# The first stage of a spectral and feed-forward kernel rewritten: the order of statistics and tables, twiddles in two parts, one PSUM pool

## The chip, the cores and the metric

The kernel runs on one core of a Trainium2 chip. A core has four computing engines, each with its own instruction stream: TensorE (PE in the profile, with PEld for its weight loads), VectorE (DVE), ScalarE (ACT) and GpSimd (POOL). SyncE (SP) issues the DMAs. An engine takes its instructions in the order of the program and waits on semaphores for the others. The metric is the device time of one execution in microseconds (us). The kernel before took 509.39 us, the median of three runs (509.39, 510.88, 509.39).

## The reference

The input is one sequence of 2048 rows with 576 columns, in bfloat16. It goes through a spectral mixing layer and a gated feed-forward layer, each with a layer norm ahead of it and a residual sum behind it:

```
def layernorm(x): return (x - mean(x)) / sqrt(var(x) + 1e-5)      # over the 576 columns

def A(x, w_r, w_i):                                # x: 1 x 2048 x 576
    X = rfft2(x, axes=(-2, -1))                    # 2048 x 289 complex
    return irfft2(X * (w_r + 1j * w_i), s=(2048, 576)).astype(bfloat16)

def B(x, w_gate, w_up, w_down):                    # 576 x 4608 twice, 4608 x 576
    return (gelu(x @ w_gate) * (x @ w_up)) @ w_down

h   = x + A(layernorm(x), A_w_r, A_w_i)
out = h + B(layernorm(h), B_w_gate, B_w_up, B_w_down)
```

## The kernel before

The 2048 rows are held as 128 partitions by 16 rows (`h_sb`, index h). The transform along the rows is done as a product of small transforms, all as matmuls with tables of sines and cosines that the kernel makes itself at its start.

**Preparation** (to about 14 us). SP loads the input in five chunks, then the spectral weights WR and WI and the first three groups of feed-forward weights (`pre`). POOL writes index patterns with iota (`iu`, `ic`, `ip`, `iD`, `iJ`, `ik`, `rev`), makes the identity, and clears DF, DI and, later, three `Zt` tiles. VectorE works out angles from them: `mu` for the 16-point table F16, `s2p` for the twiddles, `pd` and `kd` (L221 to L230) for the column tables. ACT turns angles into sines.

**First stage** (about 14 to 30 us), for the 16 rows h. The mean and variance of a row come either from VectorE (`sd`, which calls `ln_dve`: three instructions, L120 to L122; ten of the rows) or from ACT (`ln_act`: two activations that also sum, L127; rows 1, 3, 5, 7, 9, 11), after which POOL finishes them (`ln_fin`, L131 to L133). POOL also makes the reciprocal of the standard deviation for a group of rows (`ln_rstd`: an addition, L137, and a power, L138). VectorE normalises a row into `xn` (`normalise`, L141). PE multiplies it with F16 (`row16`): four matmuls into `f2t` (L261) and two small ones into `f4` (L270). `fill` (L249) adds matmuls whose results are overwritten: 30 ahead of row 0, one ahead of each of rows 1 to 11, and four ahead of the first channel. ACT moves the results from PSUM into `Bt` (`evict`, L280, two rows at a time; `evict4`, L286, four rows of the small ones). PSUM is in one pool with three double banks for `f2t` and two single ones for `f4`, closed after this stage; a second pool with four double banks follows.

The order of these calls is written out by hand, row by row (L315 to L370):

```
    sd(0, 2)                       # L325, then F16, ln_rstd(rstd, mv, 0, 4)
    norms(0, 4)                    # L338: normalise and row16 of rows 0 to 3
    ln_rstd(rstd, mv, 4, 8)
    sd(8, 10)
```

**Column tables.** `col_sin` makes the sines and cosines of the columns in DT (two of three blocks of 128 columns) and D3 (the third); DF, DI and DS are rearranged copies, some by DMA (`sine_rows`).

**Twiddles.** After the rows, VectorE works out the angles of nine channels in one piece (L373 to L376) and ACT makes the sines (L377) and, inside the loop's first turn, the cosines (L383, `twiddles`), both in TF. A DMA transposes TF into TI (L384), and another then loads `wd_a`.

**Channel loop** (L625, about 30 to 64 us), in the order 1 to 7, then 0, in which each channel c is taken together with c + 8. `f2` multiplies Bt with the column tables (L456) and moves the result to `pq` (L464: ACT, VectorE for channel 9). `f3` applies the twiddles TF (`comb`, L471 and L472) and ACT moves g and hs out (L492). `sums_of` adds and subtracts them into `xab` (L501, L502); `wmul` multiplies with WR and WI (L519 to L531) into a `Zt` tile. `i3` applies the transposed twiddles TI (L547, L549). The steps of three channels overlap: in turn i the loop issues f2 of channel i, f3 of channel i-1, wmul of channel i-2 and i3 of channel i-3. `weights()` (L404 to L407), called in the first turn, finishes WR and WI on VectorE. `late_tables()` (L410 and following) is called in the second.

**The rest.** `inv_cols` is the inverse transform of the columns (L596); after that the second layer norm, whose rows are transposed by DMA, and the feed-forward part (L848 and L868), from 78.67 us to the end.

Of the kernel before, what the change touches and what calls it, by code (L numbers as in the profile page):

```python
# [20 lines left out]
P = 128  # L21
# [20 lines left out]
def kernel_body(  # L42
# [33 lines left out]
    chunks = ((0, 2), (2, 4), (4, 8), (8, 12), (12, 16))  # L76
# [31 lines left out]
    DT = keep.tile([P, 2, 2, 2, JH], BF16, name="DT")  # L108
# [20 lines left out]
    def ln_fin(dst, h):  # L129
        sq = roll.tile([P, 1], FP32, name="sq", tag="sq", bufs=2)  # L130
        G.tensor_scalar(dst[:, h, :], sums[:, h, :], 1.0 / D, None, op0=ALU.mult)  # L131
        G.tensor_tensor(sq[:], dst[:, h, 0:1], dst[:, h, 0:1], ALU.mult)
        G.tensor_tensor(dst[:, h, 1:2], dst[:, h, 1:2], sq[:], ALU.subtract)  # L133
# [42 lines left out]
    def iota(t, pattern, base=0, cm=0):  # L176
        G.iota(t, pattern=pattern, base=base, channel_multiplier=cm, allow_small_or_imprecise_dtypes=True)

    iu, ic = tmp("iu", [P, H, 8]), tmp("ic", [P, H, 8])
# [6 lines left out]
    iota(ip[:], [[0, 1]], 0, 1)  # L186
    iD = tmp("iD", [P, 3], FP32)
# [3 lines left out]
    make_identity(nc, ident[:])  # L191
    rev = tmp("rev", [P, 1])
    iota(rev[:], [[0, 1]], 2 * P - 1, -2)
    G.memset(DF[:], 0.0)
    G.memset(DI[:], 0.0)
    ik = tmp("ik", [P, 9, P], FP32)
    iota(ik[:], [[1, 9], [16, P]])

# [18 lines left out]


    V.tensor_scalar(iD[64:128, 2:3], iD[64:128, 2:3], 192.0, None, op0=ALU.add)
    pd, kd = tmp("pd", [P, 3, JP], FP32), tmp("kd", [P, 3, JP], FP32)  # L220
    V.tensor_tensor(  # L221
        pd[:],
        iD[:, :].unsqueeze(2).to_broadcast([P, 3, JP]),
        iJ[:, :].unsqueeze(1).to_broadcast([P, 3, JP]),
        ALU.mult,
    )
    C23 = 8388608.0
    V.tensor_scalar(kd[:], pd[:], 1.0 / D, C23, op0=ALU.mult, op1=ALU.add)
    V.tensor_scalar(kd[:], kd[:], -C23, -float(D), op0=ALU.add, op1=ALU.mult)
    V.tensor_tensor(pd[:], kd[:], pd[:], ALU.add)  # L230

    def drop_sign(dst, src):
        V.tensor_scalar(
            dst[:].bitcast(I32),
            src[:].bitcast(I32),
            1,
            1,
            op0=ALU.logical_shift_left,
            op1=ALU.logical_shift_right,
        )  # L240

# [9 lines left out]
    def row16(h):  # L251
        if h % 2 == 0:
            ps_f[h] = two("f2t")
        if h % 4 == 0:
            ps_f["f4", h] = one("f4")
        f2t, f4 = ps_f[h - h % 2], ps_f["f4", h - h % 4]
        fill(f2t[:, h % 2, :], 30 if h == 0 else 1 if h < 12 else 0)
        x = xn[:, h, :]
        for t in range(2):
            for n, d0 in ((0, t * P), (1, DH + t * P)):  # L260
                T.matmul(  # L261
                    f2t[:, h % 2, t * 2 * P : (t + 1) * 2 * P],
                    lhsT=x[:, d0 : d0 + P],
                    rhs=F16[:, n : n + 2, :],
                    start=(n == 0),
                    stop=(n == 1),
                )
        o = (h % 4) * P
        for p0, d0 in ((0, 256), (64, 512)):
            T.matmul(  # L270
                f4[p0 : p0 + 64, o : o + P],
                lhsT=x[:, d0 : d0 + 64],
                rhs=F16[:, 0, :],
                start=True,
                stop=True,
            )

    def evict(*hs):
        for h in hs:
            A.copy(  # L280
                Bt[:, 0:4, :].rearrange("p t (c h l) -> p (t c) h l", c=16, h=16)[:, :, h : h + 2, :],
                ps_f[h][:].rearrange("p h (tc l) -> p tc h l", l=8),
            )

    def evict4(h):
        A.copy(  # L286
            Bt[:, 4, :].rearrange("p (c h l) -> p h c l", c=16, h=16)[:, h : h + 4, :, :],
            ps_f["f4", h][:].rearrange("p (h c l) -> p h c l", h=4, c=16),
        )
# [5 lines left out]
    def fin(*hs):  # L295
        for h in hs:
            ln_fin(mv, h)

# [5 lines left out]
    D3 = tmp("D3", [P, 2, 2, JH], BF16)  # L304
    pr, ab = tmp("pr", [P, 9, P]), tmp("ab", [P, 9, P], FP32)
# [4 lines left out]
    def col_sin(r, src, bias):  # L310
        s = src[:].rearrange("p t (a j) -> p t a j", a=2)
        A.activation(DT[:, :, :, r, :], s[:, 0:2], ACT.Sin, bias=bias[:], scale=-2.0 * PI / D)
        A.activation(D3[:, :, r, :], s[:, 2], ACT.Sin, bias=bias[:], scale=-2.0 * PI / D)

    for h in range(1, 12, 2):  # L315
        ln_act(h)
    fin(1, 3)
    for t, w in zip(wm, (A_w_r, A_w_i)):
# [6 lines left out]
    sd(0, 2)  # L325
    V.tensor_tensor(
        F16[:, 0:2, :],
        fs[:].unsqueeze(1).to_broadcast([P, 2, P]),
        mask[:].unsqueeze(1).to_broadcast([P, 2, P]),
        ALU.mult,  # L330
    )
    V.tensor_scalar(F16[:, 2, :], F16[:, 0, :], -1.0, None, op0=ALU.mult)
    ln_rstd(rstd, mv, 0, 4)
    for z in Zts:
        G.memset(z[:, :, J:], 0.0)
    sd(4, 6)
    fin(5, 7)
    norms(0, 4)  # L338
    ln_rstd(rstd, mv, 4, 8)
    sd(8, 10)  # L340
    fin(9, 11)
    col_sin(1, pd, zerob)
    drop_sign(kd, pd)
    norms(4, 6)
    evict(0)
    norms(6, 8)
    ln_rstd(rstd, mv, 8, 12)
    evict(2)
    evict4(0)
    evict(4)  # L350
    sd(14, 13)
    norms(8, 10)
    col_sin(0, kd, hpib)
    sd(12)
    norms(10, 12)
    ln_rstd(rstd, mv, 12, 14)
    sd(15)
    ln_rstd(rstd, mv, 14, 16)
    evict(6)
    evict4(4)  # L360
    evict(8)
    norms(12, 14)
    G.tensor_copy(DF[0:32], D3[0:32])
    G.tensor_copy(DF[96:128], D3[96:128])
    evict(10)
    evict4(8)
    norms(14, 16)
    evict(12)
    evict4(12)
    evict(14)  # L370


    V.tensor_scalar(pr[:], ik[:], s2p[:, 0:1], None, op0=ALU.mult)  # L373
    V.tensor_scalar(pr[:], pr[:], 2047, None, op0=ALU.bitwise_and)
    V.tensor_scalar(ab[:], pr[:], -1024.0, None, op0=ALU.add)
    drop_sign(ab, ab)  # L376
    A.activation(TF[:, :, 2, :], pr[:], ACT.Sin, bias=pib[:], scale=-2.0 * PI / S)  # L377
    V.tensor_scalar(TF[:, :, 0, :], TF[:, :, 2, :], -1.0, None, op0=ALU.mult)


    def twiddles():
        sine_rows()
        A.activation(TF[:, :, 1, :], ab[:], ACT.Sin, bias=nhpib[:], scale=2.0 * PI / S)  # L383
        nc.sync.dma_start(  # L384
            TI[:].rearrange("p k r q -> p (k r) q"), TF[:].rearrange("p k r q -> p (k r q)"), transpose=True
        )
        nc.sync.dma_start(wd_a[:], wd_view[:, 0:NWA, :])
# [41 lines left out]
    psum_pool.__exit__(None, None, None)  # L429
    psum = ctx.enter_context(tc.tile_pool(name="psum2", bufs=1, space=bass.MemoryType.PSUM))  # L430

    def two(name):
        return psum.tile([P, 2, 512], FP32, name=name, tag="two", bufs=4)

# [8 lines left out]
    order = [1, 2, 3, 4, 5, 6, 7, 0]  # L443

# [4 lines left out]
    def f2(c):  # L449
        ps = two("pq_ps")  # L450
        if c == 1:
            fill(ps[:, 0, :], 4)
# [17 lines left out]
    def comb(dst, k1, t0, a, t1, b):  # L470
        T.matmul(dst, lhsT=TF[:, k1, t0, :], rhs=a, start=True, stop=False)  # L471
        T.matmul(dst, lhsT=TF[:, k1, t1, :], rhs=b, start=False, stop=True)  # L472
# [62 lines left out]
    def i3(k, s):  # L535
# [7 lines left out]
        if k:  # L543
            pv = ps[:].rearrange("p a (n h e l) -> p (a n) e h l", n=2, h=H, l=8)
            for n, w in (((0, 0), (1, 1)), ((2, 3), (3, 4)), ((0, 2),))[s]:
                o = w * P
                T.matmul(pv[:, n], lhsT=z[:, o : o + P], rhs=TI[:, k, 1:3, :], start=True, stop=False)  # L547
                o += 2 * ZS
                T.matmul(pv[:, n], lhsT=z[:, o : o + P], rhs=TI[:, k, 0:2, :], start=False, stop=True)  # L549
# [13 lines left out]
        for n, c, j, p0, m in (  # L563
# [4 lines left out]
            for b in range(2):  # L568
                for a in range(2):
# [3 lines left out]
                        rhs=TI[:, 8 * b, 1 - a + c, :],  # L573
# [51 lines left out]
    for i in range(n + 1):  # L625
# [3 lines left out]
        if i == 0:  # L629
            twiddles()  # L630
# [14 lines left out]
        if not last:  # L645
            f2(order[i] + 8)
        if i == 0:
            weights()
# [285 lines left out]
```

## Time and profile before

| what | value |
|---|---|
| median of three runs | 509.39 us |
| time of the profiled execution | 509.37 us |
| its span in the trace | 507.2 us |
| PE busy | 494.9 us (98%) |
| VectorE busy | 214.7 us (42%) |
| ACT busy | 152.0 us (30%) |
| POOL busy | 32.6 us (6%) |
| first matmul of row 0 | 14.07 us |
| first matmul of the channel loop (f2) | 30.65 us |
| first matmul of the feed-forward part | 78.67 us |

The span runs from the first to the last record of the trace. A line of the timeline has the start in us, the duration in us, the engine, the line of the code, the operation, what it writes and reads, and how many instructions it stands for. A line of the chain of waits has start, length, engine, what is written, and the line; the chain is followed back from the last instruction to what released it.

### The profile page before, as it was taken

The numbers are of one execution on the slowest core, as the hardware profiler recorded it, in microseconds if no ns is written. First come the engines' busy times: TensorE is split into PE (matmuls) and PEld (weight loads), VectorE is DVE, ScalarE is ACT, GpSimd is POOL, SyncE is SP. The second block draws the span as 40 slices with busy tenths as digits, with TensorE's granted clock in tenths as the row PEclk, the third lists the DMA queues.
The fourth block names the chain that finished last, engine by engine and source line by source line (L and its number), as shares of the span: only waits on it lengthen the run. The fifth ranks groups of instructions, "written<-read, shape, count | busy, mean of one in ns | idle before, by whom it ended". The sixth has DMA issues, their size and how long they took to land.

```text
span 507.2 us, 9921 instructions
## 1 busy us (share of the span) xinstructions
PE 494.9 (98%) x4355; PEld 292.4 (58%) x4355; DVE 214.7 (42%) x418; ACT 152.0 (30%) x265; POOL 32.6 (6%) x81
## 2 busy tenths in 40 slices
PE   6989999999999999999999999999999999999997
PEld 2457775555557774444467744444577544444775
DVE  8979974689661015433311034433201233333001
ACT  8588984322230002333310023233200132323000
POOL 8700010111110000000000000000000000000000
PEclk9999999999999999999999999999999999999999
DMA  8985057779970019997730089978400577780000
GB/s 287 230 149 156 1 162 207 151 151 193 190 143 1 0 43 200 187 200 145 148 64 0 1 182 198 186 163 156 101 0 1 120 162 156 159 153 3 13 12 25
DMA packets 86811, 60.85 MB, mean 120 GB/s; under 512 B 22640, under 2 KB 85488, under 8 KB 86768
## 3 DMA queue, kind: packets, MB, share of 16 engines
q1 hardware_dynamic: 86480, 59.03, 57.7%
q0 software_dynamic: 288, 1.18, 0.9%
q8 instruction: 34, 0.56, 0.5%
q14 instruction: 9, 0.07, 0.1%
HBM read 52.65 MB, written 2.36 MB: 108 GB/s over the span
## 4 chain that ended last, share of the span: by engine, by line
PE 93%; DVE 4%; DMA 1%; ACT 1%; POOL 0%; issue 0%; ACTq 0%
PE gu L848 55%; PE acc L868 28%; PE f2t L261 2%; PE pq_ps L456 1%; PE cs_ps L596 1%; PE eo_ps L549 1%; PE y_ps L713 1%; PE eo_ps L547 1%; PE gh_ps L472 1%; PE f2t L249 1%; DMA Bt<-hrow 1%; PE gh_ps L471 1%; DMA h_sb<-in_A_x_dram 1%; PE f L270 1%; DVE h_sb L758 1%; DVE st L121 0%
## 5 line engine op out<-in xcount | busy, mean ns | idle before, releaser
L848 PE MATMUL gu<-Bt,wgu 64*128 64x512 bf16 x2592 | 281.5, 376 | 0.9 <-DMA Bt<-hrow 0.9
L848 PEld LDWEIGHTS <-wgu 64*128 64x128 bf16 x2592 | 130.9, 94 | 148.3 <-issue 1.9
L856 ACT ACTIVATE g_sb<-gu 128x512 f32<-128x512 f32 x144 | 86.0, 597 | 302.8 <-PE gu L848 302.8
L857 DVE TENSOR_TENSOR P_sb<-g_sb,gu 128x512 bf16<-128x512 f32 x144 | 98.7, 685 | 152.9 <-ACT g_sb L856 152.9
L868 PEld LDWEIGHTS <-P_sb 128*128 128x128 bf16 x1152 | 112.4, 98 | 30.6 <-issue 2.4
L868 PE MATMUL acc<-wd,P_sb 128*128 128x288 bf16 x768 | 99.3, 286 | 0.0
L880 DVE TENSOR_TENSOR h_sb<-h_sb,acc 128x576 bf16<-128x576 bf16 x15 | 11.3, 754 | 118.2 <-PE acc L868 118.2
L868 PE MATMUL acc<-wd_a,P_sb 128*128 128x288 bf16 x384 | 52.3, 286 | 0.5 <-DVE h_sb L876 0.5
L249 PE MATMUL f2t<-h_sb,ident 128*128 128x512 bf16 x41 | 13.2, 447 | 4.4 <-DMA h_sb<-in_A_x_dram 4.4
L456 PE MATMUL pq_ps<-DT,Bt 128*128 128x290 bf16 x64 | 12.4, 287 | 0.0
L738 DVE TENSOR_SCALAR hrow<-h_sb,mv,rstd 128x1152 bf16<-128x1152 bf16 x14 | 12.1, 866 | 0.0
L138 POOL TENSOR_TENSOR rstd<-rstd,mhalf 128x1 f32<-128x1 f32 (+2 forms) x17 | 11.8, 694 | 1.4
L249 PEld LDWEIGHTS <-ident 128*128 128x128 bf16 x45 | 4.9, 108 | 11.9 <-issue 5.9
L137 POOL TENSOR_SCALAR rstd<-mv 128x1 f32<-128x1 f32 (+2 forms) x17 | 4.1, 239 | 109.7 <-DVE mv L122 109.5
L596 PEld LDWEIGHTS <-EO 128*128 128x128 bf16 x96 | 9.1, 96 | 3.0 <-issue 0.2
L456 PEld LDWEIGHTS <-Bt 128*128 128x128 bf16 x96 | 9.2, 97 | 2.5
L261 PE MATMUL f2t<-F,xn 128*128 128x256 bf16 x64 | 9.7, 274 | 0.8 <-DVE xn L141 0.8
L464 ACT CAST pq<-pq_ps 128x580 bf16<-128x580 f32 x15 | 9.9, 660 | 0.9 <-PE pq_ps L456 0.8
L120 DVE BATCH_NORM_STATS2 st<-h_sb 128x6 f32<-128x288 bf16 x22 | 9.8, 444 | 0.0
L121 DVE BATCH_NORM_STATS2 st<-h_sb 128x6 f32<-128x288 bf16 x22 | 9.7, 442 | 0.0
L280 ACT CAST Bt<-f2t 128x1024 bf16<-128x1024 f32 x8 | 8.1, 1011 | 5.2 <-PE f2t L261 5.2
L596 PE MATMUL cs_ps<-DI,EO 128*128 128x290 bf16 x32 | 9.1, 285 | 0.0
(135 smaller groups left out, 263.3 us busy)
## 6 DMA issues: line engine op xcount, KB each, us to landing
wgu<-in_B_w_gate_dram SPq DMA_DIRECT2D x48, 432.0 KB, 5.2
wgu<-in_B_w_up_dram SPq DMA_DIRECT2D x48, 432.0 KB, 6.7
wd<-in_B_w_down_dram SPq DMA_DIRECT2D x2, 1728.0 KB, 7.9
h_sb<-in_A_x_dram SPq DMA_DIRECT2D x3, 576.0 KB, 5.9
wd_a<-in_B_w_down_dram SPq DMA_DIRECT2D x1, 1728.0 KB, 9.0
out_dram<-h_sb SPq DMA_DIRECT2D x3, 576.0 KB, 3.3
WR<-in_A_w_r_dram SPq DMA_DIRECT2D x1, 650.2 KB, 8.7
WI<-in_A_w_i_dram SPq DMA_DIRECT2D x1, 650.2 KB, 11.3
```

The lines of the kernel that those rows point to most:

```text
L138: G.tensor_tensor(dst[:, sl], dst[:, sl], mhalf[:, sl], ALU.pow)
L249: T.matmul(dst, lhsT=ident[:], rhs=h_sb[:, 2, 0:512], start=True, stop=True)
L261: T.matmul(f2t[:, h % 2, t * 2 * P : (t + 1) * 2 * P], lhsT=x[:, d0 : d0 + P], rhs=F16[:, n : n + 2, :], start=(n == 0), stop=(n == 1),)
L456: T.matmul(ps[:, par, 0:JP], lhsT=Bt[:, t, col], rhs=DT[:, t // 2, par] if t < 4 else DF[:, par], start=(t == par), stop=(t == 4),)
L464: (V.tensor_copy if c == 9 else A.copy)(sb[:].rearrange("p r (j a) -> p r j a", a=2), ps[:, :, 0:JP].rearrange("p a (r j) -> p r j a", r=2),)
L596: T.matmul(ps[:, e, 0:JP], lhsT=EO[x][:, 2 * e + jt if jt < 2 else 4, 2 * g : 2 * g + 2].rearrange("p h e k l -> p (h e k l)"), rhs=DI[:, ...
L738: V.tensor_scalar(hrow[:], h_sb[:, h, :].rearrange("p (r k) -> p r k", k=64).unsqueeze(2).to_broadcast([P, NR, 2, 64]), mv2[:, h, 0:1], rs ...
L848: T.matmul(gu[:, c, :], lhsT=w[rows, r, i * P : (i + 1) * P], rhs=hl[tcnk % 2][rows, r, :], start=(r == 0), stop=(r == NR - 1),)
L856: A.activation(g_sb[:], gu[:, 0, :], ACT.Gelu_apprx_tanh)
L857: V.tensor_tensor(p_sb(fa + i), g_sb[:], gu[:, 1, :], ALU.mult)
L868: T.matmul(acc[:, c, 0:DH], lhsT=p_sb(f)[:, st * P : (st + 1) * P], rhs=wd[f // NWA][:, f % NWA, cc], start=(f == 0), stop=(f == NFT - 1),)
L880: V.tensor_tensor(hv, hv, acc[:, :, 0:DH], ALU.add)
```

## The change

Preparation. DF, DI and the `Zt` tiles are cleared on VectorE, ahead of `mu`, instead of on POOL. The 1152-element pattern `ik` is replaced by a 9-element `kv` and a 128-element `q16`. `pd` and `kd` are made later, in two functions (`turns`, `phases`) with per-partition scalars in place of broadcast operands. The input is loaded in six chunks.

Statistics. `ln_act` scales inside the activation and sums straight into `mv`; `ln_fin` then takes two POOL instructions for two rows instead of three for each. `ln_act` calls are spread between the evictions. The first `ln_rstd` is issued ahead of POOL's two indirect DMAs instead of behind them.

Twiddles. They are made in two parts, for the channels in the order in which the loop uses them (`ts`): the first two ahead of the rows, the other seven in turns 0 to 2 of the loop. Each part has its own transposing DMA.

Rows. `fill` has 16 matmuls ahead of row 0 instead of 30, and five behind the last row instead of four in `f2(1)`. The small matmuls of rows 12 to 15 (`row16_rest`) come after the large ones; rows 14 and 15 are evicted one by one; the last `evict4` and the DF copies are on VectorE. D3 becomes the third block of DT, so that `col_sin` is one activation. All PSUM tiles come from one pool of four double banks. `weights()` and `sine_rows()` are called ahead of the loop, and `f2(9)` follows `f2(1)` directly.

```diff
-    psum_pool = tc.tile_pool(name="psum", bufs=1, space=bass.MemoryType.PSUM)
-    psum = psum_pool.__enter__()
+    psum = ctx.enter_context(tc.tile_pool(name="psum", bufs=1, space=bass.MemoryType.PSUM))
...
-        return psum.tile([P, 2, 512], FP32, name=name, tag="two", bufs=3)
-
-    def one(name):
-        return psum.tile([P, 512], FP32, name=name, tag="one", bufs=2)
+        return psum.tile([P, 2, 512], FP32, name=name, tag="two", bufs=4)
...
-    chunks = ((0, 2), (2, 4), (4, 8), (8, 12), (12, 16))
+    chunks = ((0, 2), (2, 4), (4, 6), (6, 8), (8, 12), (12, 16))
...
     def ln_act(h):
-        for i, fn in ((0, ACT.Identity), (1, ACT.Square)):
+        for i, fn, sc in ((0, ACT.Identity, 1.0 / D), (1, ACT.Square, 1.0 / D**0.5)):
             junk = roll.tile([P, D], BF16, name="junk", tag="junk", bufs=2)
-            A.activation(junk[:], h_sb[:, h, :], fn, accum_out=sums[:, h, i : i + 1])
...
+            A.activation(junk[:], h_sb[:, h, :], fn, scale=sc, accum_out=mv[:, h, i : i + 1])
+
+    def ln_fin(hs):
+        sq = roll.tile([P, H], FP32, name="sq", tag="sq", bufs=2)
+        G.tensor_tensor(sq[:, hs], mv[:, hs, 0], mv[:, hs, 0], ALU.mult)
+        G.tensor_tensor(mv[:, hs, 1], mv[:, hs, 1], sq[:, hs], ALU.subtract)
...
+    V.memset(DF[:], 0.0)
+    V.memset(DI[:], 0.0)
+    for z in Zts:
+        V.memset(z[:, :, J:], 0.0)
...
+    kv = tmp("kv", [P, 9], FP32)
+    iota(kv[:, 0:7], [[1, 7]], 1)
+    iota(kv[:, 7:9], [[8, 2]])
+    q16 = tmp("q16", [P, P], FP32)
+    iota(q16[:], [[16, P]])
+    make_identity(nc, ident[:])
...
-    G.memset(DF[:], 0.0)
-    G.memset(DI[:], 0.0)
-    ik = tmp("ik", [P, 9, P], FP32)
-    iota(ik[:], [[1, 9], [16, P]])
...
+    def angle_a(sl):
+        n = sl.stop - sl.start
+        V.scalar_tensor_tensor(
+            pr[:, sl],
+            q16[:].unsqueeze(1).to_broadcast([P, n, P]),
+            s2p[:, 0:1],
+            ks[:, sl].unsqueeze(2).to_broadcast([P, n, P]),
+            op0=ALU.mult,
+            op1=ALU.add,
+        )
+        V.tensor_scalar(pr[:, sl], pr[:, sl], 2047, None, op0=ALU.bitwise_and)
+
+    def angle_b(sl):
+        V.tensor_scalar(ab[:, sl], pr[:, sl], -1024.0, None, op0=ALU.add)
+        drop_sign(ab[:, sl], ab[:, sl])
...
+    def turns():
+        for t in range(3):
+            V.tensor_scalar(kd[:, t, :], iJ[:], iDs[:, t : t + 1], C23, op0=ALU.mult, op1=ALU.add)
+        V.tensor_scalar(kd[:], kd[:], -C23, -float(D), op0=ALU.add, op1=ALU.mult)
+
+    def phases():
+        for t in range(3):
+            V.scalar_tensor_tensor(
+                pd[:, t, :], iJ[:], iD[:, t : t + 1], kd[:, t, :], op0=ALU.mult, op1=ALU.add
+            )
...
+        fill(f2t[:, b, :], 16 if h == 0 else 1 if h < 12 else 0)
...
+        if h < 12:
+            row16_rest(h)
...
+    first, rest = slice(0, 2), slice(2, 9)
+    angle_a(first)
+    angle_b(first)
+    ln_act(1)
+    ln_act(3)
+    sine(first)
+    cosine(first)
+    sd(0)
+    row_table()
+    sd(2)
+    ln_fin(slice(1, 4, 2))
+    ln_rstd(rstd, mv, 0, 4)
...
+    turns()
+    minus_sine(first)
+    turn_tf(first)
+    ln_act(5)
+    ln_act(7)
+    norms(0, 4)
     sd(4, 6)
-    fin(5, 7)
-    norms(0, 4)
+    ln_fin(slice(5, 8, 2))
     ln_rstd(rstd, mv, 4, 8)
+    evict(0, 2)
+    evict4(0)
+    ln_act(9)
+    phases()
+    norms(4, 8)
+    drop_sign(kd[:], pd[:])
+    ln_act(11)
+    evict(4, 6)
+    evict4(4)
+    col_sin(1, pd, zerob)
     sd(8, 10)
...
+    ln_fin(slice(9, 12, 2))
     ln_rstd(rstd, mv, 8, 12)
...
+    sd(12, 13)
+    ln_rstd(rstd, mv, 12, 14)
+    norms(8, 12)
+    sd(14, 15)
+    ln_rstd(rstd, mv, 14, 16)
+    evict(8)
     col_sin(0, kd, hpib)
...
     evict(10)
     evict4(8)
...
+    norms(12, 16)
+    V.tensor_copy(DF[0:32], D3[0:32])
+    V.tensor_copy(DF[96:128], D3[96:128])
+    for h in range(12, 16):
+        row16_rest(h)
+    evict(12, 14, 15)
+    fill(two("f2t")[:, 0, :], 5)
...
         V.tensor_copy(WR[:, 9 : H + 1, 0:J], wm[0][:].rearrange("p (r j) -> p r j", r=8))
+        evict4(12)
...
+    weights()
+    sine_rows()
...
         if i == 0:
-            twiddles()
+            f2(order[0] + 8)
+            angle_a(rest)
...
                 sums_of(order[0])
+                sine(rest)
+                angle_b(rest)
             else:
+                if i == 2:
+                    cosine(rest)
+                    minus_sine(rest)
+                    turn_tf(rest)
+                    nc.sync.dma_start(wd_a[:], wd_view[:, 0:NWA, :])
                 wmul(order[i - 2], i - 1, order[i - 1])
```

More of the change, by code (lines that the diff above doesn't have):

```diff
@@ L310, in col_sin @@
     def col_sin(r, src, bias):
[L311 to L317, printed above, removed]
+        A.activation(
+            DT[:, :, :, r, :],
+            src[:].rearrange("p t (a j) -> p t a j", a=2),
+            ACT.Sin,
+            bias=bias[:],
+            scale=-2.0 * PI / D,
+        )
+    first, rest = slice(0, 2), slice(2, 9)
[10 more added lines that the diff above has]
+    ln_rstd(rstd, mv, 0, 4)
     for t, w in zip(wm, (A_w_r, A_w_i)):
@@ L324, in kernel_body @@
         )
[L325 to L335, printed above, removed]
+    turns()
[4 more added lines that the diff above has]
+    norms(0, 4)
     sd(4, 6)
-    fin(5, 7)
-    norms(0, 4)
+    ln_fin(slice(5, 8, 2))
@@ L374, in kernel_body @@
[L374 to L387, printed above, removed]
+    norms(12, 16)
@@ L644, in kernel_body @@
             i3(order[i - 3], 1)
-        if not last:
+        if not last and i:
             f2(order[i] + 8)
-        if i == 0:
-            weights()
         if i >= 3:
```

121 lines of the change are left out of this document (47 added, 74 removed).

## The prediction

> **What bounds the kernel now.** I read the page's summary first, then the chain of waits, the timeline of the first 45 us, and last a table of busy time by stage. The page gives the profiled execution a span of 507.2 us; its own time is 509.37 us, 0.02 us below the median of the three runs (509.39), so a shift worked out in this trace is added to the median as it stands.
>
> The share of busy time says that TensorE (PE) is busy 98% of the span. From 78.67 us on (the feed-forward part, which the change does not touch) it hardly waits. So the change is worth only the shift of what comes before. This is the table by stage (start and end; length; busy us and instructions of PE, PEld, DVE = VectorE, ACT, POOL; clock; DMA share; GB/s):
>
> ```profile
> 4.35:14.07 9.72, 8.88 (x30) 3.33 (x30) 9.21 (x25) 8.61 (x26) 8.56 (x15) 1.00 1.07 319
> 14.07:28.20 14.13, 14.13 (x107) 7.77 (x107) 13.21 (x36) 9.48 (x12) 8.73 (x22) 1.00 1.10 228
> 28.20:35.40 7.20, 5.15 (x38) 3.47 (x40) 4.46 (x9) 6.17 (x8) 0.00 (x0) 1.00 0.60 102
> 47.40:51.10 3.70, 3.70 (x32) 2.83 (x31) 3.67 (x9) 3.47 (x7) 0.00 (x0) 1.00 0.00 0
> ```
>
> In the first row PE only runs its 30 warming matmuls; VectorE works. In the second PE is full. In the third nobody is: it is a chain of hand-overs. In the fourth, one turn of the channel loop, PE and VectorE are both full, 3.70 us a channel. So from the loop's start to the feed-forward part nothing can catch up, and a shift of the loop's start goes into the total one to one. The chain shows that start:
>
> ```profile
> 13.60 0.43 DVE xn L141
> 14.07 0.61 PE f2t L261 x4
> 28.24 0.59 ACT Bt L286
> 28.83 0.92 ACT Bt L280
> 29.79 1.02 PE pq_ps L249 x4
> 30.82 0.76 PE pq_ps L456 x6
> 32.29 1.16 ACT TF L383
> 35.42 0.47 DVE xab L501
> 35.89 0.37 DVE xab L502
> 36.40 1.36 DVE m L519 x2
> 40.15 0.28 PE eo_ps L549
> ```
>
> The first normalised tile goes to PE at 14.07; the last Bt eviction ends at 29.75; the first channel matmul (f2) starts at 30.65; the cosine table (L383) holds f3 until 33.50. From xab at 35.42 VectorE runs without a gap through the first wmul, whose m starts at 36.31 (timeline), to the Zt that PE waits for (40.15). **36.31 is the mark I forecast**: after it VectorE and PE do the same work in both kernels.
>
> **The change, part by part.**
>
> Start of VectorE. The memsets of DF, DI and three Zts move from POOL to VectorE, ahead of mu. No row has a VectorE memset of that size. Low end: nothing, since mu waits until 1.70 anyway. High end, and taken: the POOL rows, 0.52 us from start to start for DF and DI, 0.16 for a Zt, 1.52 in all; mu starts at 1.01+1.52 = 2.53 instead of 1.70, +0.83. The four mu steps took 1.12: 3.65.
>
> In exchange a stall goes:
>
> ```profile
> 2.74 1.23 DVE L209 TENSOR_SCALAR iu<-iu 128x128 int32<-128x128 int32 x1
> 2.79 0.58 POOL L194 MEMSET DF<- 128x580 bf16 x1
> 3.31 0.58 POOL L195 MEMSET DI<- 128x580 bf16 x1
> 3.84 1.17 POOL L177 IOTA ik<- 128x1152 f32 x1
> 4.00 1.09 DVE L211 TENSOR_SCALAR mask<-iu 128x128 f32<-128x128 int32 x1
> ```
>
> iu and mask end 0.08 us after DI and ik do (3.97 and 5.09). Afterwards POOL has neither memsets nor ik, but kv twice and q16 (0.1 and 0.16 from the other iotas' steps), so it ends near 3.2, before iu. Then iu 0.25, mask 0.25, and six one-column steps (ia, s2a, s2p, new ks, iD, new iDs) at 0.19, their spacing at 5.15 to 5.53: 5.3. pd and kd (5.79 to 9.19, 3.4 us) no longer stand ahead of sd(0). angle_a(first) and angle_b(first) do: one two-input step on 256 elements like F at L326 (0.43) and three of 0.30 (0.16 fixed plus 0.52 ns an element, from the 870- and 1152-element TENSOR_SCALAR rows, 0.62 and 0.76): sd(0) at 6.6 instead of 9.19.
>
> First tiles. sd 0.97 and 0.93, row_table 0.54: mv of row 2 at 9.05. ln_rstd(0,4) is now ahead of both indirect DMAs on POOL, which held it until 11.99; it takes 0.36+1.07+0.1: 10.6. ACT is early enough: ln_act(3) ends near 6.7. VectorE fills the time with turns (3 x 0.31, and 0.66) and minus_sine (0.25): 10.9. So norms(0,4) start at 10.9 and PE 0.55 later, 11.45 instead of 14.07, a gain of 2.6. The 16 warming matmuls need about 11 x 0.43 + 5 x 0.21 = 5.8 us from 4.35 and end at 10.2.
>
> The rest of the rows. Here the bound changes from PE to VectorE, as PE's 16 rows need 14.1 us but the steps on VectorE are now in line: norms(0,4) 1.43, sd(4,6) 1.9, phases 3 x 0.4: 15.4; rstd(4,8) (sd(6) ended 14.25, plus 1.5) lets norms(4,8) start at 15.75; 1.4, drop_sign 0.6, sd(8,10,12,13) 3.8: norms(8,12) start at 21.55 and PE's row 8 at 22.1, which was 21.74 before. **The 2.6 us are gone at row 8.** PE then needs 3.54 for rows 8 to 11 (0.72 + 3 x 0.94) and 4 x 0.54 for the rest without their small matmuls: 27.8; row16_rest 4 x 0.18: 28.5; five warming matmuls 1.07: 29.6. ACT meanwhile: evict(10) at 25.65 to 26.6, evict4(8), evict(12), evict(14), evict(15) at 0.55, 0.95, 0.52, 0.55: 29.2. evict4(12) on VectorE, 28.7 to 29.3. So f2(1) starts at **29.6 instead of 30.65, gain 1.05**: the single PSUM pool lets the warming matmuls run beside the evictions, and the last eviction is short.
>
> Hand-overs. f2(1) and f2(9) 0.74+0.95, pq(9) on VectorE 0.76 and 0.05: f3(1) at 32.1, with its sine and cosine long there, where it waited 0.46 before. From f3 to xab 1.92, as in the chain: 34.0 instead of 35.42, gain 1.4. angle_a(rest) (896 elements, two inputs, 1.1 from pd's 1.07 for 870; then 0.66) runs on VectorE 32.05 to 33.9, behind pq(9) and just ahead of xab, so free. weights() (1.6 us, before at 33.01 to 34.70) and the two DF copies (0.66 each on POOL; about 0.25 here, from the DI copy's 0.23) stand on VectorE between its last norm (near 26.8; norms 14 and 15 wait for rstd(14,16) but come before PE asks) and f2: it waits for PE there, so nothing.
>
> Off the path, at nothing: ln_fin now has two POOL steps a pair of rows instead of six, but the rstd behind it waits for VectorE's statistics; col_sin is one ACT instruction instead of two and has 1.5 us between evict(8) and evict(10); the third and fourth f4 tile now share the PSUM slots of f2t, and each slot asked for was evicted over 1 us before (row 6 needs evict4(0), done near 16.6, and starts near 18).
>
> What the loop takes back. Between xab and m now stand angle_b(rest), 2 x 0.66, and minus_sine(rest), 0.43. Before: 36.31-35.42 = 0.89. After: 0.75+1.32+0.14+0.43 = 2.64. So m starts at 34.0+2.65 = **36.65 instead of 36.31: +0.35 us**. ACT gets sine(rest) and cosine(rest), 1.0 us each (1.27 x 7/9). hs(2) ends at 38.25, before VectorE asks for it at 38.9; cosine, pq(11), pq(4) follow, f3(3,0) starts near 39.9 and is done when Zt comes at 40.5. ACT has 0.2 us to spare a turn. Price 0, 0.3 at the high end.
>
> SP. The first transpose (6 blocks) waits behind the weight loads, whose last issue ended at 21.6; the five sine-row DMAs come after it, landed 11 us from issue, wanted at 57. The second (21 blocks) is issued near 39.5 instead of 33.47; with 6.1 us to land it is there at 45.6, and channel 3 asks for it at 47.46. wd_a goes behind it, 37.77 to about 43, 9 us to land, wanted after 150. h_sb in six chunks costs SP 0.46 us of issue (2.29/5), seen by no one. All at nothing, covered by these distances.
>
> Sum: -1.05 (f2) -0.35 (no wait for the cosine) +1.75 (steps moved into the loop) = **+0.35 us: 509.7 us.** What can't be read from a row: VectorE memsets from 0 (-0.55, as POOL then holds iu to 3.3) to 0.1 more; one-column steps at 0.13 (-0.35); turns and phases at 0.26 a piece (-0.4); warming matmuls hidden (-0.4); rstd waits gone (-0.2); angle steps (-0.2). All together -2.1: 507.6. Upward: POOL's power slowed as at 16.05 (1.39 for 1.04, +0.35) ahead of rows 0 and 4, ACT 0.3, memsets 0.1: +1.1, 510.8.
>
> [...] The power step at 16.05 ran 1.39 us while VectorE's kd (L233, 0.56 us for 870 elements, no longer than its like) ran inside it: VectorE was not held, POOL was. Memset, iota and copy are another matter: iu and mask above, and norms(14,15), 1.48 us beside POOL's DF copy where two norms take 0.72. [...]
>
> **Rivals.**
>
> *Slower, by POOL.* If VectorE and POOL exclude each other as memset and iu did, rstd(0,4) (0.27+1.07) goes in series with turns instead of beside them, and the later power steps with phases and norms. Place: between sd(2) and row 0. Price: 1.3 us on VectorE, which bounds everything after: 511.0. For it: the 1.23 us row; against it: the L233 row. It decides once a single power step holds VectorE for its length.
>
> *Slower, by the clock.* PE now idles before row 4 (1 us) and, after its warming matmul, before row 8 (row 7 ends 20.0, row 8 at 22.1: 1.9 us). The warming matmuls ran at 0.43 us for 4.65 us, then 0.21. If the new gap throws the clock back, rows 8 to 12 run at half speed for 4.65 us: +2.3, 512.0. Against it: the gap of 1.59 us before 29.79 left the next matmuls at 0.21, and the granted clock is 1.00 in every stage. [...]
>
> *Faster.* VectorE's terms are at their low ends, as listed: 507.6. For it: const memsets start 0.03 us apart and independent one-column steps 0.07 (L770 to L771), so several of mine may overlap. Against: angles and statistics each wait for the one before, and the statistics' 0.95 us a row is measured ten times.
>
> **How the numbers follow.** No change within 0.3% (1.5 us, about what a measurement of this kernel can tell from none: the three runs span 1.49) has 0.54; its own range 508.2 to 510.8. Slower 0.25 (POOL 0.15, clock 0.05, a wait not seen 0.05); faster 0.21. The range for 8 in 10 takes the low ends and the POOL rival in: 507.6 to 511.4.
>
> **What would show it.** Right: iu and mask near 0.25 us; first xn near 10.9; idle PE before rows 4 and 8, released by VectorE; f2 near 29.6, m near 36.65. Wrong: PE without gaps between rows 0 and 15; VectorE held during rstd; matmuls of 256 columns spaced 0.22 instead of 0.13 after row 8; m of the first wmul outside 35.2 to 37.8, or turns of the loop longer than 3.70.

## The result, and the profile after

The changed kernel takes 508.21 us, the median of 20 runs (508.17 to 509.70); the kernel before, on the same chips, 509.33 (509.03 to 510.88). The ratio is 0.9977, with a 95% interval of 0.9969 to 0.9985: 0.23% faster, about 1.1 us. That lies inside the range given and inside "no change within 0.3%", but the forecast was 0.35 us slower: its sign was wrong. Of both kernels some executions (4 of 20 after, 6 of 20 before) take 1 to 1.6 us longer than the rest; what these are in the changed kernel is a question of the experiments, in the kernel before it stays open.

The profiled execution took 508.19 us, with a span of 506.4. This is one line of the page of the changed kernel: the large matmuls of the rows, with the idle time of PE ahead of them (4.8 us), which was 0.8 us before.

```profile
L306 PE MATMUL f2t<-F,xn 128*128 128x256 bf16 x64 | 9.3, 273 | 4.8 <-DVE xn L137 4.8
```

The table by stage of the changed kernel, with the columns of the one before (stage; length; busy us and instructions of PE, PEld, DVE, ACT, POOL; clock; DMA share; GB/s):

```profile
11.10:16.40 5.30, 3.92 (x28) 2.06 (x29) 4.71 (x14) 2.86 (x4) 3.86 (x6) 1.00 1.15 233
16.40:22.00 5.60, 3.93 (x29) 2.08 (x30) 5.46 (x18) 5.36 (x12) 1.93 (x5) 1.00 1.08 277
22.00:28.00 6.00, 5.99 (x52) 3.71 (x53) 5.28 (x16) 4.71 (x7) 1.94 (x4) 1.00 1.12 224
28.00:33.30 5.30, 5.30 (x41) 3.51 (x40) 4.18 (x9) 3.37 (x7) 0.00 (x0) 1.00 1.13 108
47.40:51.10 3.70, 3.70 (x33) 2.83 (x31) 3.67 (x9) 3.42 (x7) 0.00 (x0) 1.00 0.21 70
```

The rows from row 0 to the start of row 8 (first and second line) leave PE idle for a quarter of the time or more (1.38 of 5.30 us, 1.67 of 5.60). VectorE idles 0.59 us in the first, 0.52 of them ahead of row 4, where it waits for POOL's rstd, and 0.14 in the second: VectorE's line, with that one step of POOL in it, is the bound there, as the prediction said, where PE was before. From row 8 on PE is full again, now also in the stretch behind the rows, where it had stood for 2 of 7.2 us. A turn of the loop is still 3.70 us.

The chain of waits of the changed kernel, in part (start, length, engine, what is written, line):

```profile
10.61 1.65 DVE xn L137 x4
14.71 1.18 POOL rstd L134
21.63 0.31 DVE xn L137
21.99 0.61 PE f2t L306 x4
27.96 1.19 PE f2t L294 x5
29.15 2.24 PE pq_ps L483 x18
34.10 0.54 DVE ab L249
34.67 0.63 DVE ab L225
35.44 0.33 DVE TF L259
```

The two Bt evictions and the cosine table that stood in the chain before are gone from it, and the three steps that the change moved into the loop (34.10, 34.67, 35.44) are in it. The marks, in us:

| mark | before | forecast | after |
|---|---|---|---|
| first statistics sd(0) | 9.19 | 6.6 | 6.33 |
| row 0 on PE | 14.07 | 11.45 | 11.10 |
| row 8 on PE | 21.74 | 22.1 | 21.99 |
| f2, first channel matmul | 30.65 | 29.6 | 28.98 |
| xab | 35.42 | 34.0 | 33.27 |
| m of the first wmul | 36.31 | 36.65 | 35.69 |
| first matmul of the feed-forward part | 78.67 | 79.0 | 77.97 |
| last addition | 504.11 | 504.46 | 503.41 |

(The last two forecasts are the shift of 0.35 at m carried on.) The trace shows 0.70 us less up to the last addition. The span is 0.8 shorter. The remaining 0.3 lies outside it: time less span has a median of 2.13 us in the runs of the kernel before and 1.80 in those of the changed one.

### The profile page after: what moved, and what is told of

Its sections match the earlier page's. It is cut to its first block, busy times and chain, and to the rows that moved or that the text cites. A ratio compares the mean times of both kernels' runs of the same rounds, so it can differ in the third digit from the quotient of the medians.

```text
span 506.4 us, 9895 instructions
## 1 busy us (share of the span) xinstructions
PE 491.3 (97%) x4342; PEld 291.2 (57%) x4342; DVE 215.6 (43%) x436; ACT 151.2 (30%) x265; POOL 24.2 (5%) x64
## 4 chain that ended last, share of the span: by engine, by line
PE 91%; DVE 5%; DMA 1%; ACT 1%; POOL 1%; issue 0%; POOLq 0%; DVEq 0%
PE gu L881 55%; PE acc L901 28%; PE pq_ps L483 2%; DMA wd<-in_B_w_down_dram 1%; PE cs_ps L623 1%; PE eo_ps L576 1%; PE f2t L306 1%; PE eo_ps L574 1%; DVE xn L137 1%; PE gh_ps L499 1%; ACT cwb L636 1%; DVE st L118 1%; PE y_ps L746 1%; DVE st L117 1%; PE gh_ps L498 1%; POOL rstd L134 0%
## 5 line engine op out<-in xcount | busy, mean ns | idle before, releaser
L294 PE MATMUL f2t<-h_sb,ident 128*128 128x512 bf16 x32 | 10.5, 434 | 4.4 <-DMA h_sb<-in_A_x_dram 4.4
L483 PE MATMUL pq_ps<-DT,Bt 128*128 128x290 bf16 x64 | 12.4, 287 | 0.0
L306 PEld LDWEIGHTS <-xn 128*128 128x128 bf16 x64 | 5.9, 98 | 7.7 <-DVE xn L137 6.1
L330 ACT CAST Bt<-f2t 128x1024 bf16<-128x1024 f32 (+1 forms) x9 | 8.1, 927 | 5.0 <-PE f2t L306 5.0
L498 PE MATMUL gh_ps<-pq,TF 128*128 128x289 bf16 x32 | 8.7, 286 | 0.6 <-ACT TF L256 0.6
```

The costliest lines, as they stand in the source:

```text
L306: T.matmul(f2t[:, b, t * 2 * P : (t + 1) * 2 * P], lhsT=x[:, d0 : d0 + P], rhs=F16[:, n : n + 2, :], start=(n == 0), stop=(n == 1),)
L483: T.matmul(ps[:, par, 0:JP], lhsT=Bt[:, t, col], rhs=DT[:, t // 2, par] if t < 4 else DF[:, par], start=(t == par), stop=(t == 4),)
L498: T.matmul(dst, lhsT=TF[:, ts[k1], t0, :], rhs=a, start=True, stop=False)
```

## The experiments

The theory: the changed kernel's rows are bound by VectorE's line of statistics, tables and norms, so PE's own work there has slack; the gain is made behind the last row, where warming matmuls and small matmuls run beside the evictions; the loop takes part of it back one to one, through the angle steps between xab and m. The rivals: that the gain comes from PE's fewer warming matmuls, from POOL (the statistics, the rstd ahead of the indirect DMAs) or from the memsets; and that gaps on PE cost clock. All are compared with the kernel before at 509.3 us and, by marks, with the changed kernel; each edit is to the changed kernel unless said otherwise.

**30 warming matmuls again, ahead of row 0.**

```diff
-        fill(f2t[:, b, :], 16 if h == 0 else 1 if h < 12 else 0)
+        fill(f2t[:, b, :], 30 if h == 0 else 1 if h < 12 else 0)
```

> The changed kernel with 30 instead of 16 warming matmuls ahead of row 0. They end near 12.4 us instead of 9.4 (14 more at 0.215), so row 0 starts at about 12.4 instead of 11.10. Theory (VectorE bounds rows 4 to 15, PE has 1.4 us idle before row 4 and 1.7 before row 8): row 8 stays at 22.0, f2 at 29.0, time 508.2. Rival (PE's work and the lower number of warming matmuls is what gained): everything 1.3 us later, 509.5.

Measured: 511.43 us (510.76 to 511.79), ratio 1.0036 [1.0024, 1.0048]. Both theories missed it. The matmuls ended at 13.79, not 12.4, so row 0 was 2.7 us late. The first 12 follow one another by 0.42 us, up to 9.55; in the profiled run of the changed kernel only the first seven do by 0.43, up to 7.28, and those behind by 0.22. From the 9.3 us that all 30 take I estimate 13 or 14 slow ones, seven more than there, which cost 1.5 us. Row 8 was 1.7 us late too, at 23.70, though VectorE's line does not need PE. The timeline of ACT and, after it, of POOL in this run shows the way:

```profile
18.15 0.59 ACT L336 CAST Bt<-f 128x512 bf16<-128x512 f32 x1
18.62 0.70 ACT L124 ACTIVATE junk<-h_sb 128x576 bf16<-128x576 bf16 x1
```
```profile
22.15 1.04 POOL L134 TENSOR_TENSOR rstd<-rstd,mhalf 128x4 f32<-128x4 f32 x1
```

The statistics of rows 9 and 11 (L124) stand on ACT behind the evictions of rows 0 to 3; late rows make late evictions, late statistics, and the rstd of rows 8 to 11 at 22.15 instead of 20.26; VectorE waited 1.58 us for it. So PE's slack is about 1 us, up to ACT's queue, and not free. PE then idled 2.26 us ahead of row 8, and the clock in 24 to 27 us was 0.50: another 1.5 us.

**No warming matmuls between the rows.**

```diff
-        fill(f2t[:, b, :], 16 if h == 0 else 1 if h < 12 else 0)
+        fill(f2t[:, b, :], 16 if h == 0 else 0)
```

> The changed kernel without the single warming matmul ahead of each of rows 1 to 11. Theory (VectorE bounds): rows 8 to 11 go faster by 3 x 0.32, but rows 12 to 15 wait for VectorE's norms (26.08 for row 14), so the last row ends near 27.5 as now and the time stays at 508.2, within 0.3. Rival (the clock is held up by them): row matmuls of 256 columns spaced 0.22 instead of 0.13 somewhere, 509 to 510.5. Rival (PE bounds): f2 1 us earlier, 507.2.

Measured: median 508.64, lowest 508.16, ratio 0.9986 [0.9972, 1.0000]. Two lines of PE's timeline and one stage of the profiled run (18 to 21 us; the clock is the third number from the end):

```profile
16.40 0.84 PE L306 MATMUL f2t<-F,xn 128*128 128x256 bf16 x4 [2.35 <-DVE xn L137]
21.98 0.61 PE L306 MATMUL f2t<-F,xn 128*128 128x256 bf16 x4 [1.27 <-DVE xn L137]
```
```profile
18.00:21.00 3.00, 2.71 (x17) 1.14 (x14) 2.90 (x11) 1.50 (x3) 1.17 (x3) 0.66 1.00 272
```

After a gap of 2.35 us the clock fell, to 0.66 in this stage and 0.77 in the one before it, and the large matmuls of rows 4 to 7 took up to 1.03 us a row instead of 0.60; yet row 8 (21.98), f2 (28.98) and m (35.69) did not move, and the time was 508.27. PE has that slack ahead of row 8: VectorE bounds the rows. Half of the runs took 0.8 to 1.9 us more, as the rival on the clock had it.

**The moved angle steps done twice.**

```diff
                 angle_b(rest)
+                angle_b(rest)
...
                     minus_sine(rest)
+                    minus_sine(rest)
```

> The changed kernel with angle_b(rest) and minus_sine(rest) each done twice, on VectorE between xab and the first m. They take 1.19 and 0.33 us in the trace of the changed kernel. Theory (what stands there goes into the time one to one): m at 37.2 instead of 35.69, time 509.7 (+1.5). Rival (VectorE has slack there, and the loop's pace is PE's): less than +0.7, under 508.9.

Measured: 511.3 (510.89 to 513.05), ratio 1.0044 [1.0028, 1.0060]. f2 stayed (28.97), m moved from 35.69 to 37.46, +1.77 (expected +1.5): these steps pass into the loop's start one to one. The feed-forward part moved more, +3.05, because PE idled 1.95 us at 40.92 and the clock was 0.50 in 42 to 45 us.

**Two PSUM pools, as before.** The warming matmuls then stand in the second pool.

```diff
-    psum = ctx.enter_context(tc.tile_pool(name="psum", bufs=1, space=bass.MemoryType.PSUM))
+    psum_pool = tc.tile_pool(name="psum", bufs=1, space=bass.MemoryType.PSUM)
...
-    fill(two("f2t")[:, 0, :], 5)
...
+    psum_pool.__exit__(None, None, None)
+    psum = ctx.enter_context(tc.tile_pool(name="psum2", bufs=1, space=bass.MemoryType.PSUM))
...
+    fill(two("f2t")[:, 0, :], 5)
```

> The changed kernel with the two PSUM pools of before (three double and two single banks, closed after the rows; then four double banks), and the five warming matmuls at the head of the second pool. Theory (the gain arises behind the last row, where the single pool lets warming matmuls run beside the evictions): the warming matmuls start only after the last eviction, near 28.9, f2 at about 29.95 instead of 28.98, time 509.15 (+0.95). Rival (the pools do not matter, the short last evictions do): f2 within 0.3 us of 28.98, 508.2 to 508.5.

Measured: 4 of 10 runs at 509.25 to 509.32, 6 at 510.67 to 510.81; ratio 1.0005 [0.9990, 1.0020]. The rows are unchanged; PE's timeline behind them:

```profile
28.88 1.24 PE L298 MATMUL f2t<-h_sb,ident 128*128 128x512 bf16 x5 [0.93 <-ACT Bt L334]
29.96 0.41 PE L494 MATMUL pq_ps<-DT,Bt 128*128 128x290 bf16 x2
```

f2 comes 0.98 us later, m 1.04, the feed-forward part 0.99, and the lower group of runs 1.05. As expected: the single pool is worth 1 us, nearly the whole of the 1.1 us gained and more than the 0.70 that the trace shows.

**POOL's rstd behind the indirect DMAs again.**

```diff
-    ln_rstd(rstd, mv, 0, 4)
     for t, w in zip(wm, (A_w_r, A_w_i)):
...
+    ln_rstd(rstd, mv, 0, 4)
```

> The changed kernel with POOL's two indirect DMAs back ahead of the first ln_rstd. POOL then issues them from about 6.9 to 9.5, and the first rstd ends near 11.0 instead of 10.57; VectorE is through with turns and minus_sine at 10.45, so norms(0,4) start at 11.05 instead of 10.61. Theory (VectorE's line bounds the rows, so what delays it at row 0 delays all): row 8, f2 and the time +0.45, 508.65. Rival (the gaps before rows 4 and 8 swallow it): row 8 within 0.15 of 21.99, 508.2.

Measured: median 510.77, lowest 509.29, ratio 1.0027 [1.0013, 1.0042]. The two issues hold POOL longer than I assumed (timeline of POOL):

```profile
7.55 1.24 POOL L375 DMA_INDIRECT wm_r<-in_A_w_r_dram,rev  x1 [0.65 <-issue]
9.10 1.35 POOL L375 DMA_INDIRECT wm_i<-in_A_w_i_dram,rev  x1 [0.30 <-DVE mv L119]
10.83 1.06 POOL L134 TENSOR_TENSOR rstd<-rstd,mhalf 128x4 f32<-128x4 f32 x1
```

Row 0 came at 12.41 instead of the expected 11.55, row 8 1.1 us late, and the lowest time is 1.1 us higher: of the 1.3 us that the late rstd costs at row 0, VectorE's line passes 1.1 on. In the profiled run the clock also fell, behind a gap of 1.67 us, to 0.50 in 24 to 27 us.

**All twiddles ahead of the rows.**

```diff
-    first, rest = slice(0, 2), slice(2, 9)
+    first = slice(0, 9)
...
-            angle_a(rest)
...
-                sine(rest)
-                angle_b(rest)
...
-                    cosine(rest)
-                    minus_sine(rest)
-                    turn_tf(rest)
```

> The changed kernel with the twiddles of all nine slots ahead of the rows, none in the loop. VectorE: the two-input step 1.45 instead of 0.42, three steps of 0.80 instead of 0.32, minus_sine 0.49 instead of 0.22: +2.7 ahead of row 0. Theory (both stages are bounded by VectorE, so it is an exchange): f2 +2.7 (31.7); between xab and m 1.52 us less; m at 36.9, time +1.2, 509.4. Rival (the idle before row 0 is PE's and ACT's, and VectorE's extra work there is hidden): f2 within 0.5 of 28.98 and the time below 507.5.

Measured: 511.57, lowest 510.05, ratio 1.0046 [1.0033, 1.0059]. Row 0 is at 13.55 (+2.45), row 8 at 24.93 (+2.94), f2 at 31.93 (+2.95; forecast +2.7), m at 37.11 (+1.42). PE idled 4.28 us ahead of row 0, the clock fell to 0.81 and 0.62 in the stages of 12 to 18 us, and the 0.5 us more at row 8 are again a wait of VectorE (0.56 us) for an rstd whose statistics stood behind late evictions on ACT. So the split costs 1.5 us on VectorE behind f2 and saves 3 ahead of it, about 2.4 of them on VectorE alone, and the feed-forward part comes 1.8 us earlier by it.

**Two shortenings: the rows, and the angles.** The first gives row 4's statistics to ACT, and moves the indirect DMAs and one table step:

```diff
+    ln_act(4)
...
+    ln_fin(slice(4, 5))
+    norms(0, 4)
+    sd(6)
...
-    norms(0, 4)
-    sd(4, 6)
...
+    drop_sign(kd[:], pd[:])
     norms(4, 8)
-    drop_sign(kd[:], pd[:])
```

> The changed kernel with VectorE's line through the rows made shorter: statistics of row 4 on ACT (idle from 9.84 to 12.68), the indirect DMAs behind ln_rstd(4,8), drop_sign ahead of norms(4,8), where VectorE waits 0.52 us. Theory (VectorE's line bounds the rows): row 4 at 15.4 instead of 16.40, row 8 at 20.75 instead of 21.99, f2 at 27.8 instead of 28.98, time 507.0 (-1.2). Rival (PE, or ACT's evictions, bound it): f2 within 0.3 of 28.98, 508.2.

The second splits `angle_a` into its two steps, with the first ahead of pq(9), and calls `angle_b(rest)` ahead of xab:

```diff
         if i == 0:
+            angle_0(rest)
             f2(order[0] + 8)
-            angle_a(rest)
+            angle_1(rest)
+            angle_b(rest)
...
                 sine(rest)
-                angle_b(rest)
```

> The changed kernel with the first angle step of the late twiddles ahead of pq(9), where VectorE waits 0.97 us for PE, and angle_b(rest) ahead of xab instead of behind it: 1.19 us less between xab and the first m. Theory (what stands there goes into the time one to one, until ACT's line, with the sine and the cosine, is the next bound): m near 34.75 instead of 35.69; f3 of channel 3 still waits for the cosine and pq(11) until 38.5, so i3 starts at 39.1 instead of 39.52: time 507.4 to 507.8. Rival (VectorE's extra steps were free): 508.2.

Measured: lowest 507.34 and 507.32, medians 508.70 and 508.67; ratios 0.9978 [0.9966, 0.9989] and 0.9976 [0.9964, 0.9987]. Each shortens its part: f2 is at 28.01 in the first (-0.97, expected -1.2; a late indirect DMA then held VectorE for 1.48 us ahead of 29.27, and of the 0.97 only 0.51 are left at xab, 32.76); xab to m takes 1.28 instead of 2.42 us in the second. But 6 of 10 runs of each were about 1.3 us longer, so neither median beats the changed kernel. The profiled run of the second is one of those, and shows why (PE's timeline, then two stages of 3.41 us):

```profile
21.97 0.61 PE L308 MATMUL f2t<-F,xn 128*128 128x256 bf16 x4 [1.67 <-DVE xn L137]
22.92 0.85 PE L308 MATMUL f2t<-F,xn 128*128 128x256 bf16 x4
```
```profile
19.72:23.13 3.41, 1.75 (x13) 0.93 (x13) 3.34 (x12) 2.42 (x3) 2.45 (x4) 1.00 1.06 293
23.13:26.54 3.41, 3.41 (x17) 1.54 (x15) 2.73 (x10) 1.94 (x2) 1.03 (x2) 0.50 1.13 183
```

The gap is the changed kernel's, whose profiled run kept 0.60 us a row behind it. Here the clock fell during row 9, at 23.13, for 3.41 us; f2 came at 30.44, 1.46 later, and the run was 1.48 longer than the lowest.

**The gaps filled.** Five warming matmuls ahead of row 4, seven ahead of row 8.

```diff
-        fill(f2t[:, b, :], 16 if h == 0 else 1 if h < 12 else 0)
+        fill(f2t[:, b, :], {0: 16, 4: 5, 8: 7}.get(h, 1 if h < 12 else 0))
```

> The changed kernel with five warming matmuls ahead of row 4 and seven ahead of row 8 instead of one each, inside the gaps of 1.4 and 1.7 us in which PE waits for VectorE. Theory (the +1.5 us of some executions of the changed kernel, 4 of 20, is the clock falling at rows 8 to 11 after these gaps): the usual time stays at 508.2 and no or hardly any execution is above 509. Rival (that +1.5 has another place, which these matmuls do not touch): the same share of executions, one in five to one in two, near 509.7.

Measured: 508.20 (508.14 to 508.53, 11 runs), ratio 0.9979 [0.9970, 0.9988]. The marks are those of the changed kernel; PE idles 0.53 and 0.38 us ahead of the two rows:

```profile
16.40 0.61 PE L306 MATMUL f2t<-F,xn 128*128 128x256 bf16 x4 [0.53 <-DVE xn L137]
21.98 0.61 PE L306 MATMUL f2t<-F,xn 128*128 128x256 bf16 x4 [0.38 <-DVE xn L137]
```

None of 11 runs was long. Against the 4 of 20 of the changed kernel alone that could be chance (one time in twelve); but of four kernels with gaps of 1.6 to 1.7 us ahead of row 8, 20 of 50 were: 4 of 20 (the changed kernel), 6 of 10 (each of the shortenings) and 4 of 10 (memsets, below). The first shortening has a gap of only 0.47 us ahead of row 4. So it is the gap ahead of row 8 that makes the long runs of the changed kernel, and warming matmuls in VectorE's shadow end them at no cost. No long run of the changed kernel itself was profiled; that of the second shortening stands for it.

**The memsets on POOL again**, those of the Zt tiles too.

```diff
-    V.memset(DF[:], 0.0)
-    V.memset(DI[:], 0.0)
...
+    G.memset(DF[:], 0.0)
+    G.memset(DI[:], 0.0)
```

> The changed kernel with DF, DI and the Zt tiles cleared on POOL again, DF and DI behind rev, the Zt tiles behind the first ln_rstd and the indirect DMAs. VectorE's mu starts at 1.70 instead of 2.57, but POOL clears from 3.2 to 4.3 and holds iu or mask until then. [...] Rival (the memsets are pure cost on VectorE): sd(0) at 5.5, time 507.4. Beside it: the time less the span, 2.12 us in the kernel before and 1.80 in the changed one, shows whether clearing on POOL makes that difference (2.1) or not (1.8).

Measured: 508.37, ratio 0.9996 [0.9986, 1.0005], 6 of 10 runs at 508.30 to 508.41. sd(0) came at 6.03, between the 6.33 of the changed kernel and the 5.5 of the rival: iu is not held (0.21 us) and mask by little (0.35 us instead of 0.23), but the step `ks` ends with the clearing of DI and takes 0.56 us instead of 0.23. Row 0 came 0.3 us earlier too, at 10.80, but row 4 0.13 later, since its rstd on POOL now stands behind the clearing of the Zt tiles, and with it row 8 0.12 later (22.11) and m 0.13. The move is worth about 0.1 us, and it is not where the time outside the span went (1.81 us here).

**The statistics alone, in the kernel before.** Only the new `ln_act` and `ln_fin`, 12 POOL instructions fewer.

```diff
-        for i, fn in ((0, ACT.Identity), (1, ACT.Square)):
+        for i, fn, sc in ((0, ACT.Identity, 1.0 / D), (1, ACT.Square, 1.0 / D**0.5)):
...
-    def ln_fin(dst, h):
+    def ln_fin(hs):
```

> The kernel before with one part of the change alone: ln_act sums straight into mv and ln_fin takes two POOL instructions for two rows instead of three for each (12 POOL instructions fewer). Theory (PE bounds the rows of the kernel before, POOL's rstd waits for VectorE's statistics): row 0 at 14.07, f2 at 30.65 and the span at 507.2 as before. The time less the span, 2.12 us before and 1.80 in the changed kernel, is not explained so far. Theory A (it goes with the number of POOL instructions): about 1.9, time 509.1. Theory B (it does not): 2.12, 509.3.

Measured: 508.99 (508.95 to 510.30), ratio 0.9997 [0.9988, 1.0007]. f2 is at 30.32, 0.33 earlier than in the profiled run of the kernel before, where no shift was expected; at the feed-forward part 0.19 of it is left, and the lowest times of the two kernels are alike (508.95 and 508.98). Time less span stayed at 2.12 us: the statistics on POOL are not what the changed kernel saves outside the span.

**Together.** Both shortenings, the indirect DMAs right behind `rev`, and two and six warming matmuls ahead of rows 4 and 8.

```diff
+        fill(f2t[:, b, :], {0: 16, 4: 2, 8: 6}.get(h, 1 if h < 12 else 0))
```

> The changed kernel with both shortenings: through the rows (row 4's statistics on ACT, drop_sign ahead of norms(4,8), the indirect DMAs behind rev, where POOL is idle from 3.2, so that the weights are there in time), in the hand-over (first angle step ahead of pq(9), angle_b(rest) ahead of xab), and two and six warming matmuls ahead of rows 4 and 8. Theory: row 8 at 21.0 (-1.0), f2 at 28.0 (-1.0), another -0.85 in the hand-over; 506.4 and no execution 1.5 us above. Rival (the early indirect DMAs delay the input's chunks or VectorE's tables): row 0 later than 11.4, time 507.3 or more.

Measured: 506.64 (506.61 to 506.66, 5 runs), ratio 0.9950 [0.9936, 0.9964]: 2.7 us less than before and 1.6 less than the changed kernel. PE's timeline and, after it, VectorE's:

```profile
28.18 0.41 PE L488 MATMUL pq_ps<-DT,Bt 128*128 128x290 bf16 x2
```
```profile
33.74 0.75 DVE L551 TENSOR_TENSOR m<-xab,WR 128x1156 bf16<-128x1156 bf16 x1
```

f2 is 0.80 us earlier than in the changed kernel and m 1.95, with PE idle 0.53 us ahead of row 8; the feed-forward part begins at 76.29, 1.68 earlier.

## Why the prediction was right and wrong

*Start of VectorE: right.* The memsets took 1.48 us (forecast 1.52), mu began at 2.57 (forecast 2.53), and the stall of iu and mask is gone. Row 0 came 0.35 earlier than forecast, 0.27 of it because sd(0) did.

```profile
3.39 0.22 DVE L210 TENSOR_SCALAR iu<-iu 128x128 int32<-128x128 int32 x1
3.64 0.23 DVE L212 TENSOR_SCALAR mask<-iu 128x128 f32<-128x128 int32 x1
8.79 0.88 DVE L271 TENSOR_SCALAR kd<-iJ,iDs 128x290 f32<-128x290 f32 x3
9.71 0.61 DVE L272 TENSOR_SCALAR kd<-kd 128x870 f32<-128x870 f32 x1
```

*"The 2.6 us are gone at row 8": right.* Row 8 came at 21.99 (forecast 22.1), with PE idle 1.39 us ahead of row 4 and 1.67 ahead of row 8, both released by VectorE. Without warming matmuls the rows did not move, and with POOL's rstd later they moved by most of its delay, as a line on VectorE that waits for that rstd must. What the prediction did not see is the way back from PE: rows more than about 1 us late delay ACT's evictions and statistics, and through them the next rstd.

*f2, "gain 1.05": the term that was mis-sized.* It was 1.67. Of the 0.62 us, row 8 and the rows behind it give 0.13, rows 12 to 15 0.12 (2.04 for 2.16), and "row16_rest 4 x 0.18" 0.36: the eight small matmuls, back to back, take 0.36 us from start to start of what follows (27.55 to 27.91), where I had priced them at the 0.18 a pair that they take behind the large ones. The evictions, which f2 also needs, had to come in as well: they ended at 28.83 on ACT and 28.77 on VectorE, where the prediction had 29.2 and 29.3. At the forecast ends they would have held f2 to about 29.3, and half of the 0.62 would not have come. The mechanism was right: with two pools again, f2 loses 0.98.

*Hand-overs: right within 0.1.* f2 to xab takes 4.29 (forecast 4.4), with no wait for the cosine.

*"+1.75" for the steps moved into the loop: right in kind, 0.23 too much.* xab to m took 2.42 instead of 2.65: the two angle steps 1.19 for 1.32, minus_sine 0.33 for 0.43. Doubling them moved m by 1.77 and splitting them otherwise gave 1.14 back, so they are in the path one to one.

*Behind m: nothing, as said,* but for 0.08 us that came off before the feed-forward part.

So the steps that failed are sizes, above all that of the gain at f2 (1.67 us, not 1.05); that alone turns the sign. The forecast was a small difference of two large terms, -1.4 and +1.75, each somewhat wrong, and both in the same direction: 0.62 + 0.11 + 0.23 + 0.08 = 1.04 us in the trace. The other 0.5 of the profiled execution's 1.53 are 0.1 behind the last addition and 0.38 outside the span; the prediction added the shift of the trace to the median as it stands, as if the time outside the span stayed. What caused the latter stays open: not POOL's statistics, not the memsets, not the pools (1.78 us with two).

*The rivals.* POOL and VectorE excluding each other: it did not happen. The power step at 9.51 took 1.06 us (1.07 in the kernel before, at 12.35), and `turns` beside it 0.88 and 0.61 (the lines at 8.79 and 9.71), no longer than the 0.93 and 0.66 forecast. The clock: dismissed for the wrong reason. I argued from one gap of 1.59 us in the trace of before that did no harm; the runs show that a gap of 1.67 sometimes does, and costs 1.5 us rather than the 2.3 that I gave: in the profiled run of the second shortening the half clock lasted 3.41 us, not 4.65, and the run was 1.48 longer than the lowest. It did not decide the median here, with 4 of 20 runs, but it decided the medians of the two shortenings, 6 of 10 each with about the same gap: that is luck, not a margin.

## What to carry to other kernels

Where a stage's bound passes from one engine to another, forecast the marks on both sides of the stage and size the stretch behind it with care: here the rows kept their end, and the whole gain came from work that could start before the last eviction. A short idle stretch of PE in front of real work is a risk even where one trace shows the full clock, as here, where the same 1.67 us left it at 1.00 in one profiled run and stood ahead of a fall to 0.50 in another: look at several executions, and put warming matmuls into the shadow of the engine that binds. Here five and seven of them left gaps of 0.53 and 0.38 us, at no cost in time (508.20 us for 508.21), and none of 11 executions was long. When an edit seems worth nothing in the median, compare the lowest times and the clock by stage before dropping it; two such edits were worth 1.6 us together with the gaps filled.

## What the runs showed of the hardware

In the profiled runs the clock fell behind gaps of PE of 4.28, 2.35, 2.26, 1.95 and, in two of them, 1.67 us, while the same 1.67 us left it at 1.00 in the profiled run of the changed kernel, and 2.25 us ahead of row 8 in that with all twiddles early. The same kernel differs from run to run: 4 of 20 executions of the changed kernel took 1.3 to 1.5 us more, and none of 11 once the gaps were filled.

The length of a gap alone does not decide. The falls themselves are alike: in the stages of 3 us around each of the six, the clock lost adds up to 1.68 to 1.71 us, which is 3.4 us at 0.50. In the 3.41 us ahead of them PE was busy for 0.09, 0.31, 0.34, 0.37 and, twice, 0.51 of the time; but that share does not decide alone either. In the profiled run of the second shortening the whole gap ahead of row 8 lies in the stretch ahead of the fall (19.72 to 23.13, above: 1.75 us of 3.41 busy). In the changed kernel PE's busy share in the first of the same two stretches is the same, and the clock in the second is full:

```profile
19.72:23.13 3.41, 1.74 (x13) 0.92 (x13) 3.34 (x12) 2.42 (x3) 2.45 (x4) 1.00 1.03 330
23.13:26.54 3.41, 3.41 (x28) 1.95 (x26) 2.73 (x10) 2.97 (x4) 1.03 (x2) 1.00 1.14 200
```

What makes the difference between the two runs was not shown.

The time outside the traced span is not a constant: 2.13 us before, 1.80 in the changed kernel and most of its variants, 1.94 in the two with the rows shortened (row 4's statistics on ACT, the indirect DMAs moved).
